# Planning the side work of an attention pass head by head

## The chip, the cores and the metric

The kernel runs on one core of a Trainium2 chip. The metric is the device time of one launch in microseconds, as the median of several runs; a profiled execution gives the trace. The engines are named as in the profile: PE is TensorE (matrix multiplications, with PEld its weight loads), DVE is VectorE, ACT is ScalarE, POOL is GpSimd, and SP is SyncE, which here only issues transfers (DMAs).

## The reference

One layer over 2048 tokens of 1024 channels in float32, with modulation vectors that come from a condition `c`:

```python
mod = (silu(c) @ w_mod).reshape(1, 6, 1, 1024)
sa, ca, ga, sb, cb, gb = (mod[:, i] for i in range(6))
h = layernorm(x) * (1 + ca) + sa
x = x + ga * A(h)                  # attention with memory
h = layernorm(x) * (1 + cb) + sb
x = x + gb * B(h)                  # MLP across the tokens, 3584 wide
```

`A` projects to q, k, v (32 heads of 32 channels) and cuts the tokens into 4 segments of 512. Within a segment each head has causal softmax attention; the state of the earlier segments (`M`, `z`) is read with `phi(q)` and mixed in by a gate `g`; then `M` and `z` take in the segment. The result is multiplied by `wo`.

```python
for s in range(4):
    a_dot = softmax(q_s @ k_s.T * scale + mask) @ v_s
    a_mem = (phi(q_s) @ M) / (phi(q_s) @ z + 1e-6)
    out_s = g * a_mem + (1 - g) * a_dot
    M, z = M + phi(k_s).T @ v_s, z + sum(phi(k_s))
```

## The kernel before

**Precision.** Float32 products are made from two reduced-precision parts. `split` writes a rounded high part and, by a subtraction, the low part; a product is three matmuls (high by high, high by low, low by high). A "page" is one 128 x 2 x 512 tile with both parts of one eighth of the channels of a segment; there are 16 pages, two segments' worth.

**The attention passes.** The heads are worked in groups of four (`NG` = 8 groups). An iteration `t` is one group in one segment; two passes (`pr`) take segments 0 and 1, then 2 and 3, and within a pass each group has its two segments in turn: 32 iterations, 128 heads. The loop at lines 560 to 588 runs over heads, `n` from -3 to 128. At `n` it traces `scores(n)` (three banks of score matmuls, exponentials on ScalarE, causal masks and the low half of the probabilities on GpSimd), `maxima(n + 3)` (scores in the other orientation, whose row maxima VectorE takes; after every second head small transfers, `sk<-nt`, place them as extra rows of the stacked operands), `values(n - 1)` (probabilities by values) and a quarter of the projections of the iteration two later (`project(n + 8)`), whose results are stacked by transfers `sk<-sg`.

**The side work** lies in the same loop and uses buffers `raw` (three of 128 x 1024):

- *Weights.* `load_w` (line 167) loads the q, k and v weights of a group, in three parts of 512 KB. In the first pass `load_part` splits them on ScalarE and VectorE into `w` tiles (eight buffers, six per group), and `keep_w` stores the split parts in `wsp` for the second pass, which only loads them.
- *Late token tiles.* `token_tile` (line 218, every fifth head from 4) loads one of token tiles 8 to 15 into a `raw` buffer, normalizes it, transposes it on TensorE through the `s2` banks, modulates it on ScalarE and stores it transposed in `hT1`. `reload_h` (line 297, loop index `m` = `n + 8` from 59 to 66) fetches it for segments 2 and 3, in 16 pieces, and splits each into a page on VectorE and GpSimd.
- *Late modulation.* `mod_late` (line 495) computes 128 of the 4096 remaining modulation values: it loads 128 rows of transposed weights and VectorE multiplies by `scb` with a sum along the row (1024 wide). It is traced every third head from 12, 32 times. `mod_rows` transposes the sums and stores them in `modd`, once after the first 8 (the attention gate) and once after the last.
- *Output weights.* `wo_ahead` (line 549), every fifth head from 66, loads an eighth of `wo`, multiplies it by the gate (`gaw`) on GpSimd, splits it on ScalarE and VectorE and stores the parts in `wos`; they are fetched into pages from head 115 on.

**Order.** The compiler's scheduler puts each engine's instructions in an order of its own by a model of their times. The order of tracing gives the priority, so an instruction that is traced later can be issued earlier when its engine is free in the model and its operands are there. An instruction under `tc.issue_after(i)` comes behind `i` if both are on one engine. At run time each engine works in that order.

After the loop come the output projection (`out_proj`), the second normalization and the token MLP with a seven-product scheme (`mix`), which the change does not touch.

Of the kernel before, what the change touches and what calls it, by code (L numbers as in the profile page):

```python
# [7 lines left out]
F32 = mybir.dt.float32  # L8
# [10 lines left out]
P = 128  # L19
# [15 lines left out]
ML0 = 12  # L35
MLS = 3
HB = 3
WO0 = 66
WOS = 5
# [5 lines left out]
def attention_and_mlp(ctx, tc, x, wq, wkv, wo, beta, w1, b1, w2, b2, c, wm_a, wm_b, out):  # L45
# [13 lines left out]
    hT1 = dram.tile([2, NK, P, L], F32, name="hT1")  # L59
# [87 lines left out]

    def load_part(g, pr, kind, part, res):


        if pr == 0:
            r = a.tile([P, D], F32, tag="raw", bufs=3, name=f"raw{kind}{g}_{part}")
            SY.dma_start(r, (wkv if kind == "v" else wq)[g, :, 1024 * part:1024 * part + 1024])
        for i in range(2):
            w = aw.tile([P, 2, 512], F32R, tag="w", bufs=8, name=f"w{kind}{pr}_{g}_{part}_{i}")
            if pr == 0:
                split(w, r[:, 512 * i:512 * i + 512], A, V)
            else:
                SY.dma_start(w.bitcast(F32), wsp[g, 2 * part + i if kind == "v" else 4 + i])
            res[kind, 2 * part + i] = w  # L160
# [251 lines left out]
    def maxima(t, h):  # L412
# [8 lines left out]
        for i, o in ((0, x[:, 0:128]), (2, x[:, 128:512]), (1, y[:, 0:256]), (3, z)):  # L421
            T.matmul(o, q[:, 128 * i:128 * i + 128], k[:, 0:128 * i + 128], start=True, stop=True)  # L422
            V.tensor_tensor_reduce(o, o, mask[:, 384 - 128 * i:], 1.0, -3.0e38, op0=ALU.add, op1=ALU.max,  # L423
                                   accum_out=mx[:, h % 2, i:i + 1])
# [7 lines left out]
        for hh in range(2):  # L432
            sk = d["sk", h - 1 + hh]
            for part in range(2):
                SY.dma_start(sk[96 + part:97 + part, 0].bitcast(F32).rearrange("p (b n) -> p b n", n=128),
                             nt[part][4 * hh:4 * hh + 4].bitcast(F32))

    def scores(t, h):
        d = st[t]
        q, k = d["sk", h][:, 0], d["sk", h][:, 1]  # L440
# [16 lines left out]
        A.copy(ph[:, 0], p32)  # L457
        G.tensor_tensor(ph[:, 1], p32, ph[:, 0], op=ALU.subtract)  # L458
# [36 lines left out]
    def mod_late(j):  # L495
# [450 lines left out]
```

## Time and profile before

| what | value |
|---|---|
| median of 3 runs | 2334.57 us (2332.73 to 2335.44) |
| the profiled execution | 2335.82 us |
| its span, first to last instruction | 2334.1 us |
| mean granted TensorE clock | 0.979 |
| first score matmul of heads 0, 48, 68 and 108 | 108.6, 484.8, 664.6 and 942.7 us |
| weight splits of groups 2 to 7 on VectorE (36) | 120.4 to about 470 us |
| late token tiles, loads | 109.7 to 390.1 us |
| late modulation on VectorE (32 steps) | 184.7 to 645 us |
| output weights, loads | 470.9 to 620.0 us |
| reload of token tiles, loads | 499.0 to 603.6 us |

How to read the rows: a group row names line, engine, operation, `written<-read` tiles, shapes and count, then after the bar the busy us and the mean ns of one, then the engine's idle time in front of them and what ended it. A row of waits has the total us, the number of waits and the longest. Rows of stretches give for each engine the busy us and the instruction count, then the granted clock, the DMA share and GB/s.

### The profile page before, as it was taken

What the parts mean: (1) busy time and instruction counts of PE and PEld (TensorE: products, weight loads), DVE (VectorE), ACT (ScalarE), POOL (GpSimd) and SP (SyncE); (2) the same over time, 40 slices, a digit from 0 to 9 for tenths busy, and PEclk for the clock granted to TensorE, in tenths of its full rate; (3) what the DMA queues carried; (4) which work ended last, traced back from release to release, by engine and by line L of the source; (5) the groups of instructions that cost most, each with busy time, mean ns of one, the idle gap of its engine ahead of it and who ended that gap; (6) DMA issues with size and microseconds to landing.
All of it is one profiled execution on the core that took longest, in us unless ns stands there. A gap on an engine that the chain in (4) does not pass through costs nothing.

```text
span 2334.1 us, 38271 instructions
## 1 busy us (share of the span) xinstructions
PE 2242.2 (96%) x13866; PEld 1925.3 (82%) x13866; DVE 1724.3 (74%) x3838; ACT 1103.8 (47%) x2002; POOL 683.7 (29%) x683
## 2 busy tenths in 40 slices
PE   8989999898899999998999999999999999999999
PEld 7878888887789999976887887888888788888887
DVE  6677777677766666665999665598889787868687
ACT  5476776655556666654434333353335242424232
POOL 3154544567655555554001000023332000000000
PEclk9999999999999999987999999999999999999999
DMA  6856666578744444483465765365557542423233
GB/s 244 251 152 185 175 187 186 161 240 263 244 119 119 119 122 120 109 264 98 132 217 187 271 235 195 136 246 222 211 213 275 185 136 71 146 65 130 68 114 148
DMA packets 164272, 406.27 MB, mean 174 GB/s; under 512 B 17108, under 2 KB 63220, under 8 KB 155124
## 3 DMA queue, kind: packets, MB, share of 16 engines
q1 hardware_dynamic: 164084, 403.83, 52.9%
q8 instruction: 110, 1.80, 0.3%
q14 instruction: 78, 0.64, 0.1%
HBM read 232.04 MB, written 120.86 MB: 151 GB/s over the span
## 4 chain that ended last, share of the span: by engine, by line
PE 82%; DVE 8%; DMA 6%; issue 2%; ACT 1%; SPq 1%; POOL 1%; DVEq 0%; ACTq 0%; POOLq 0%
PE mx L743 43%; PE nps L184 12%; PE po L650 8%; PE qps L192 7%; PE pv L472 3%; DMA rawm<-in_wm_b_dram 2%; PE sx L422 1%; PE sz L422 1%; PE a L444 1%; PE rd L394 1%; PE up L404 1%; PE a L447 1%; DVE bU L120 1%; PE a L451 1%; PE sy L422 1%
## 5 line engine op out<-in xcount | busy, mean ns | idle before, releaser
L743 PE MATMUL mx<-bU,sp 128*128 128x512 f32 x2352 | 535.9, 389 | 3.1 <-DVE ac L750 1.4
L743 PEld LDWEIGHTS mx<-bU,sp 128*128 128x128 f32 x2352 | 440.8, 188 | 97.8 <-issue 2.2
L184 PE MATMUL nps<-wv,h 128*128 128x256 f32 x3072 | 435.7, 284 | 4.7 <-DVE h L119 3.5
L743 PE MATMUL mx<-bA,sp 128*128 128x512 f32 x1764 | 431.8, 389 | 3.2 <-DVE cc L750 1.6
L117 ACT CAST sp<-wr 128x384 fp32r<-128x384 f32 (+2 forms) x408 | 217.4, 545 | 445.2 <-PE mx L743 373.7
L184 PEld LDWEIGHTS nps<-wv,h 128*128 128x128 f32 x3072 | 401.3, 190 | 10.1 <-DVE h L119 3.9
L743 PEld LDWEIGHTS mx<-bA,sp 128*128 128x128 f32 x1764 | 330.8, 188 | 73.6 <-DVE cc L750 2.0
L458 POOL TENSOR_TENSOR ph<-p,ph 128x1280 f16<-128x1280 f32 x128 | 344.7, 2693 | 145.2 <-ACT ph L457 144.9
L120 DVE TENSOR_TENSOR sp<-wr,sp 128x384 fp32r<-128x384 f32 (+2 forms) x408 | 259.1, 646 | 34.0 <-ACT sp L117 33.8
L750 DVE TENSOR_TENSOR ac<-mx,ac 128x512 f32<-128x512 f32 x280 | 189.8, 687 | 92.2 <-PE mx L743 91.5
L192 PE MATMUL qps<-h,wq 128*128 128x512 f32 x768 | 204.5, 413 | 3.8 <-DVE r L347 3.6
L650 PE MATMUL po<-wo,ots 128*128 128x512 f32 x768 | 180.7, 396 | 4.0 <-DVE ots L120 2.2
L455 POOL TENSOR_SCALAR_AFFINE_SELECT p<-p 128x256 f32<-128x256 f32 x256 | 123.9, 492 | 185.1 <-ACT p L448 83.1
L457 ACT CAST ph<-p 128x1280 f16<-128x1280 f32 x128 | 161.0, 1258 | 33.4 <-POOL p L455 33.1
L192 PEld LDWEIGHTS qps<-h,wq 128*128 128x128 f32 x768 | 147.8, 199 | 34.9 <-issue 3.9
L650 PEld LDWEIGHTS po<-wo,ots 128*128 128x128 f32 x768 | 146.6, 192 | 35.1 <-ACT ots L117 2.4
L423 DVE CUSTOM_DVE_ANT_0 sx<-sx,mask 128x128 f32<-128x128 f32 (+1 forms) x256 | 110.3, 431 | 77.1 <-PE sx L422 75.6
L743 PE MATMUL mx<-bB,sp 128*128 128x512 f32 x588 | 164.3, 389 | 0.0
L472 PE MATMUL pv<-vp,ph 128*128 128x97 bf16 (+1 forms) x2560 | 150.6, 206 | 8.4 <-DVE mv L131 4.8
L472 PEld LDWEIGHTS <-ph 128*128 128x128 f16 x2560 | 118.4, 100 | 33.0 <-issue 16.7
L750 DVE TENSOR_TENSOR cc<-mx,cc 128x512 f32<-128x512 f32 x140 | 94.8, 684 | 46.8 <-PE mx L743 43.9
L743 PEld LDWEIGHTS mx<-bB,sp 128*128 128x128 f32 x588 | 110.4, 188 | 22.9
(173 smaller groups left out, 3219.2 us busy)
## 6 DMA issues: line engine op xcount, KB each, us to landing
sk<-sg SPq DMA_DIRECT2D x384, 128.0 KB
wr<-in_w_dram SPq DMA_DIRECT2D x28, 1024.0 KB
wr<-in_w_dram SPq DMA_DIRECT2D x32, 768.0 KB
bstu<-ucd SPq DMA_DIRECT2D x28, 768.0 KB
wsp<-wv SPq DMA_DIRECT2D x32, 512.0 KB
rawm<-in_wm_b_dram SPq DMA_DIRECT2D x32, 512.0 KB
wv<-wsp SPq DMA_DIRECT2D x32, 512.0 KB
pcd<-cc SPq DMA_DIRECT2D x14, 1024.0 KB
```

What stands on the lines that cost most here:

```text
L117: A.copy(hi, src)
L120: lo_eng.tensor_tensor(lo, src, hi.bitcast(F32), op=ALU.subtract)
L184: T.matmul(ps[:, aa], h[:, j, 128 * tt:128 * tt + 128], wt[:, i, o:o + 256], start=(n == 0), stop=(n >= 6 * NK - 2), skip_group_check=True)
L192: T.matmul(ps, wt[:, i, o:o + 128], h[:, j], start=(k + n == 0), stop=(3 * k + n == 3 * NK - 1))
L423: V.tensor_tensor_reduce(o, o, mask[:, 384 - 128 * i:], 1.0, -3.0e38, op0=ALU.add, op1=ALU.max, accum_out=mx[:, h % 2, i:i + 1])
L455: G.affine_select(w, w, pattern=[[0, 2], [1, 128]], compare_op=ALU.is_ge, fill=0.0, base=0, channel_multiplier=-1)
L457: A.copy(ph[:, 0], p32)
L458: G.tensor_tensor(ph[:, 1], p32, ph[:, 0], op=ALU.subtract)
L472: T.matmul(pv[:, i, 0:w], ph[:, part, o:o + 128], d["vp"][:, j, h, 0:w], start=(n == 0), stop=(n == 19), skip_group_check=True)
L650: T.matmul(ps, os_[:, i, P * ct:P * ct + P], wop[ct, nh][:, j], start=(n == 0), stop=(n == 3 * NK - 1))
L743: T.matmul(ps, ops[q][:, i, P * k:P * k + P], b[:, j], start=(m == 0 and first), stop=(m == 3 * nk - 1), skip_group_check=True)
L750: V.tensor_tensor(d, ps, d, op=ALU.add)
```

## The change

Each piece of side work is divided into a load and its work, and both are given a head: `later(n, fetch, (m, step), ...)` puts the load at head `n` and each step at head `m`. At the end of the loop's body for `n`, the pieces of that head are traced under `behind(n)`: on ScalarE, GpSimd, VectorE and SP they come behind the last instruction of that head's own work on that engine (the cast of the probabilities, the low half, the last maximum, the last `sk<-nt` transfer). TensorE has no such mark.

| side work | load at head | work at head |
|---|---|---|
| token tile i (0 to 7), now loaded into `gaw` | 5i | 5i + 2 |
| weights of group g (2 to 7), from 8g - 16 on | + 1, + 3, + 5 | + 4, + 6, + 7 (store + 7) |
| modulation j (0 to 31) | 40 + 2j | 40 + 2j + 1 and + 2 |
| output weights i (0 to 7) | 65 + 6i | 65 + 6i + 2 |

The modulation step is four multiply-and-sum instructions of 256 columns, two at each head, and a reduction of the four sums. The multiplication, split and copy of the output weights go in halves. The token tiles are split before they are stored (copy on ScalarE, subtraction on GpSimd, two stores), `hT1` has both parts, and `reload_h` is one transfer of 512 KB into the page. The gate's row is spread over `gaw` at head 62, as before.

```diff
-    hT1 = dram.tile([2, NK, P, L], F32, name="hT1")
+    hT1 = dram.tile([2, NK, P, 2, L], F32, name="hT1")
...
+    def fetch_part(g, kind, part):
+        r = a.tile([P, D], F32, tag="raw", bufs=3, name=f"raw{kind}{g}_{part}")
+        SY.dma_start(r, (wkv if kind == "v" else wq)[g, :, 1024 * part:1024 * part + 1024])
+        return r
+
+    def split_part(g, kind, part, r):
+
+        for i in range(2):
+            w = aw.tile([P, 2, 512], F32R, tag="w", bufs=8, name=f"w{kind}0_{g}_{part}_{i}")
+            split(w, r[:, 512 * i:512 * i + 512], A, V)
+            W[0, g][kind, 2 * part + i] = w
...
     def token_tile(tt):
 
-        r = a.tile([P, D], F32, tag="raw", bufs=3, name=f"rawx{tt}")
-        SY.dma_start(r, x[P * tt:P * tt + P])
+        r = gaw
         norm_x(a, r)
...
+        hi = a.tile([P, D], F32, tag="raw", bufs=3, name=f"hix{tt}")
+        A.copy(hi.bitcast(F32R), r)
+        G.tensor_tensor(r.bitcast(F32R), r, hi, op=ALU.subtract)
         i = tt % 4
-        SY.dma_start(hT1[tt // 4 - 2, :, :, P * i:P * i + P].rearrange("k p n -> p k n"),
-                     r.rearrange("p (k n) -> p k n", k=NK))
+        for part, t in enumerate((hi, r)):
+            SY.dma_start(hT1[tt // 4 - 2, :, :, part, P * i:P * i + P].rearrange("k p n -> p k n"),
+                         t.rearrange("p (k n) -> p k n", k=NK))
...
     def reload_h(seg, ct):
-        t = pj.tile([P, L], F32, tag="tmp", bufs=2, name=f"hre{seg}_{ct}")
-        SY.dma_start(t, hT1[seg - 2, ct])
         pg = new_page(f"h{seg}_{ct}")
-        split(pg, t, V, G)
+        SY.dma_start(pg.bitcast(F32), hT1[seg - 2, ct])
         hpages[seg, ct] = pg
...
+    @contextmanager
+    def behind(n):
+
+        with ExitStack() as s:
+            for e in "AGVS":
+                if (n, e) in marks:
+                    s.enter_context(tc.issue_after(marks[n, e].ins))
+            yield
...
+    def mod_part(j, r, half):
+
+        if half == 0:
+            mpart[0] = const.tile([P, 4], F32, tag="mpart", bufs=2, name=f"mpart{j}")
+        for i in (2 * half, 2 * half + 1):
+            c = slice(256 * i, 256 * i + 256)
+            V.scalar_tensor_tensor(r[:, c], r[:, c], 1.0, scb[:, c], op0=ALU.mult, op1=ALU.mult,
+                                   accum_out=mpart[0][:, i:i + 1])
+        if half == 0:
+            return
+        V.tensor_reduce(mcol[:, j:j + 1], mpart[0], axis=AX.X, op=ALU.add)
...
+    def wo_split(i, r):
+
+        nh, c2 = i // 4, 2 * (i % 4)
+        hi = a.tile([P, 2, 512], F32, tag="raw", bufs=3, name=f"woh{i}")
+        for j in range(2):
+            G.tensor_tensor(r[:, j], r[:, j], gaw[:, 512 * nh:512 * nh + 512], op=ALU.mult)
+            A.copy(hi[:, j].bitcast(F32R), r[:, j])
+            V.tensor_tensor(r[:, j].bitcast(F32R), r[:, j], hi[:, j], op=ALU.subtract)
...
+    for j in range(32):
+        n = 40 + 2 * j
+        later(n, lambda j=j: mod_fetch(j), (n + 1, lambda r, j=j: mod_part(j, r, 0)),
+              (n + 2, lambda r, j=j: mod_part(j, r, 1)))
...
-        if 4 <= n < 44 and n % 5 == 4:
-            token_tile(8 + n // 5)
-        if n >= ML0 and (n - ML0) % MLS == 0 and (n - ML0) // MLS < 32:
-            mod_late((n - ML0) // MLS)
+        with behind(n):
+            for f in todo.pop(n, ()):
+                f()
```

More of the change, by code (lines that the diff above doesn't have):

```diff
@@ L146, in attention_and_mlp @@
     raw_w = {}
+    def fetch_part(g, kind, part):
[7 more added lines that the diff above has]
+            W[0, g][kind, 2 * part + i] = w
     def load_part(g, pr, kind, part, res):
         if pr == 0:
-            r = a.tile([P, D], F32, tag="raw", bufs=3, name=f"raw{kind}{g}_{part}")
-            SY.dma_start(r, (wkv if kind == "v" else wq)[g, :, 1024 * part:1024 * part + 1024])
+            split_part(g, kind, part, fetch_part(g, kind, part))
+            return
         for i in range(2):
             w = aw.tile([P, 2, 512], F32R, tag="w", bufs=8, name=f"w{kind}{pr}_{g}_{part}_{i}")
[L156 to L159, printed above, removed]
+            SY.dma_start(w.bitcast(F32), wsp[g, 2 * part + i if kind == "v" else 4 + i])
             res[kind, 2 * part + i] = w
@@ L575, in attention_and_mlp @@
             reload_h(seg, ct + 1)
-        if n == WO0 - 4:
-            spread(gaw, 0)
-        if n >= WO0 and (n - WO0) % WOS == 0 and (n - WO0) // WOS < 8:
-            wo_ahead((n - WO0) // WOS)
         if 4 * NI - 5 <= m < 4 * NI + 3:
```

60 lines of the change are left out of this document (42 added, 18 removed).

## The prediction

> **What bounds the kernel now.** I read the page first, then the busy time of the engines by stretches, then the groups and the waits of the two stretches that lose time, and last one stall in the timeline.
>
> ```profile
> span 2334.1 us, 38271 instructions
> PE 2242.2 (96%) x13866; PEld 1925.3 (82%) x13866; DVE 1724.3 (74%) x3838; ACT 1103.8 (47%) x2002; POOL 683.7 (29%) x683
> ```
>
> TensorE is busy for 96% of the span, so only its idle time and its slow clock can be won. Side work (weight splits, late token tiles, late modulation, output weights) runs beside the attention heads, so I cut the head loop where its density changes. Each row below is one stretch; the columns are its length, the busy time and instruction count of PE, PEld, DVE, ACT and POOL, the granted clock, the DMA share and GB/s. The second set counts the first score matmul of each head (line 444) alone, so its first x is the number of heads.
>
> ```profile
> 108.60:484.80 376.20, 346.92 (x2971) 313.32 (x2970) 277.40 (x771) 257.20 (x484) 189.72 (x188) 0.96 0.61 181
> 484.80:664.60 179.80, 158.24 (x1282) 140.89 (x1281) 135.58 (x352) 94.98 (x164) 126.65 (x106) 0.92 0.72 219
> 664.60:942.70 278.10, 278.00 (x2518) 256.64 (x2517) 168.06 (x587) 174.41 (x309) 155.81 (x179) 1.00 0.47 124
> ...
> 108.60:484.80 376.20, 21.32 (x48) 9.38 (x48) 0.96 0.61 181
> 484.80:664.60 179.80, 8.88 (x20) 4.06 (x21) 0.92 0.72 219
> 664.60:942.70 278.10, 17.48 (x40) 7.57 (x41) 1.00 0.47 124
> ```
>
> The third stretch (heads 68 to 107) has no side work: TensorE never rests, its clock is 1.00, and a head takes 278.10 / 40 = 6.95 us. That is the floor. The first stretch (heads 0 to 47) also transposes eight token tiles on TensorE:
>
> ```profile
> 108.60:484.80 376.20, 10.58 (x64) 8.03 (x64) 0.96 0.61 181
> ```
>
> So it loses 376.2 - 48 x 6.95 - 10.6 = 31.9 us, and the second (heads 48 to 67) 179.8 - 20 x 6.95 = 40.8 us. Together **72.7 us** are to be had; everything else in the change lies beside a busy TensorE.
>
> Who makes TensorE wait? First its waits, stretch one and then two, then those of VectorE for transfers (us in total, times, longest):
>
> ```profile
> PE sx L422 <- DVE mx L423: 14.7, 11, 3.8
> ...
> PE sx L422 <- DVE mx L423: 9.6, 6, 4.5
> ...
> DVE rawm L498 <- DMA rawm<-in_wm_b_dram: 10.7, 7, 3.3
> DVE st L125 <- DMA rawx<-in_x_dram: 4.1, 2, 2.1
> ...
> DVE rawm L498 <- DMA rawm<-in_wm_b_dram: 7.6, 7, 2.9
> DVE h L119 <- DMA hre<-hT: 2.9, 2, 1.9
> ```
>
> TensorE waits for VectorE's row maxima: the score banks of a later head come free late because VectorE, which works in order, stands behind side work, or behind side work whose data has not landed. The costliest stall, read in the timeline (start, duration, engine, line, and in brackets the idle time before):
>
> ```profile
> 635.70 1.38 SPq L497 DMA_DIRECT2D rawm<-in_wm_b_dram  x2
> ...
> 640.52 1.23 DVE L498 SCALAR_TENSOR_TENSOR rawm<-rawm,scb 128x1024 f32<-128x1024 f32 x1 [2.94 <-DMA rawm<-in_wm_b_dram]
> 640.76 3.45 POOL L458 TENSOR_TENSOR ph<-p,ph 128x1280 f16<-128x1280 f32 x1 [1.24 <-ACT ph L457]
> 641.87 3.42 DVE L498 SCALAR_TENSOR_TENSOR rawm<-rawm,scb 128x1024 f32<-128x1024 f32 x1
> 645.62 0.69 PE L422 MATMUL sx<-sk 96*128 96x384 f32 x1 [4.47 <-DVE mx L423]
> ```
>
> A load issued at 635.70 lands at 640.52 (4.8 us); VectorE waits 2.94 us for it, then a second modulation step, 1.23 us by itself, takes 3.42 us because GpSimd's subtraction runs at the same time. TensorE pays 4.47 us, and the clock afterwards.
>
> A stall costs more than its length:
>
> ```profile
> 494.00:508.00 14.00, 11.39 (x71) 9.46 (x70) 11.71 (x31) 7.76 (x15) 8.27 (x7) 0.76 0.61 187
> ...
> PE sy L422 <- DVE mx L423: 2.3, 1, 2.3
> ```
>
> In these 14 us the longest wait is 2.3 us, and the granted clock is 0.76. The Trainium skill, "TensorE: Matmul & The Clock Gate", section on HAM oscillation, says to keep TensorE's idle gaps under some 3.4 us. By that rule short stalls would cost no clock; this row shows 2.3 us costing it, so the measurement decides, and I let the clock part shrink only with the stalls.
>
> **The change part by part.** VectorE's load per head, busy plus its waits for transfers, is what I carry through: clean 168.06 / 40 = 4.20 us; stretch one (277.40 + 10.7 + 4.1) / 48 = 6.09; stretch two (135.58 + 7.6 + 2.9) / 20 = 7.30, above the 6.95 us that TensorE needs. The losses per head are 0, 0.66 and 2.04 us. The terms, from the groups of VectorE (busy us, mean ns), stretch one and then two:
>
> ```profile
> L498 DVE SCALAR_TENSOR_TENSOR rawm<-rawm,scb 128x1024 f32<-128x1024 f32 x18 | 26.1, 1448 | 10.7 <-DMA rawm<-in_wm_b_dram 10.7
> L120 DVE TENSOR_TENSOR wv<-rawv,wv 128x512 fp32r<-128x512 f32 x22 | 31.8, 1455 | 9.0 <-ACT wv L117 9.0
> L120 DVE TENSOR_TENSOR wq<-rawq,wq 128x512 fp32r<-128x512 f32 x12 | 12.8, 1074 | 0.6 <-ACT wq L117 0.6
> L498 DVE DVE_READ_ACCUMULATOR rawm<-rawm,scb 128x1 f32 x18 | 1.4, 80 | 0.0
> L556 DVE TENSOR_TENSOR wor<-wor,woh 128x1024 fp32r<-128x1024 f32 x1 | 1.2, 1216 | 0.0
> ...
> L498 DVE SCALAR_TENSOR_TENSOR rawm<-rawm,scb 128x1024 f32<-128x1024 f32 x14 | 23.2, 1660 | 7.6 <-DMA rawm<-in_wm_b_dram 7.6
> L119 DVE CAST h<-hre 128x512 fp32r<-128x512 f32 x16 | 17.8, 1110 | 2.9 <-DMA hre<-hT 2.9
> L556 DVE TENSOR_TENSOR wor<-wor,woh 128x1024 fp32r<-128x1024 f32 x8 | 12.7, 1587 | 2.2 <-ACT woh L555 2.0 <-DMA sk<-sg 0.2
> ```
>
> *Quarters.* The smallest and middle modulation step and the nearest shorter row of the same kind:
>
> ```profile
> L498 DVE SCALAR_TENSOR_TENSOR rawm<-rawm,scb x32: 1204/1226/3418, 184.7 to 641.9; 128x1024 f32<-128x1024 f32 x32
> ...
> L368 DVE SCALAR_TENSOR_TENSOR pq<-qps,rq 128x512 f32<-128x512 f32 x6 | 4.1, 688 | 0.8 <-ACT rq L366 0.7
> L475 DVE RECIPROCAL pv<-pv 128x4 f32<-128x4 f32 x46 | 8.7, 189 | 13.8 <-PE pv L472 13.8
> ```
>
> From 688 ns at 512 columns to 1226 at 1024 is 538 per 512, so 256 columns cost about 688 - 269 = 419 ns. Four, four reads of the accumulator (80 each) and a small reduction (bounded by the 189 ns row) are 2.19 us, against 1.31 now: 0.9 us more on each of 32. The means above the 1226 ns add up to 26.1 + 23.2 - 32 x 1.226 = 10.1 us of waiting for GpSimd. Quartered, that is between 10 us (one wait per step, as now) and 40 us (one per quarter); I take 20, nearer the low end since two quarters stand back to back. So 32 x 2.19 + 20 = 90 us, 2.8 us each. With steps every second head from 40 on, 4 fall in stretch one (now 18), 10 in two (now 14), 18 in three (now 0).
>
> *Stored split segments.* The 16 reloads lose VectorE's casts (17.8 + 2.9 us of waiting) and GpSimd's subtractions; each becomes one transfer straight into the page. In exchange each token tile gets a 1024-wide copy on ScalarE, a 1024-wide subtraction on GpSimd and a second store; the nearest rows are GpSimd's 1024-wide multiply (2510 ns) and the share of stretch one: 8 x 2.5 = 20 us on a GpSimd that is busy for 189.72 of 376.20, so at nothing; without that cover, 20 us at most.
>
> ```profile
> L120 POOL TENSOR_TENSOR h<-hre,h 128x512 fp32r<-128x512 f32 x16 | 20.5, 1279 | 7.7 <-DVE h L119 5.5 <-PE a L447 2.2
> L554 POOL TENSOR_TENSOR wor<-wor,gaw 128x1024 f32<-128x1024 f32 x7 | 17.6, 2510 | 8.4 <-DMA wor<-in_wo_dram 8.4
> ```
>
> *Output weights.* Now eight steps around heads 48 to 67, after it one there and seven later, in halves, about 1.6 us each as now. This also takes seven loads and their stores out of the stretch with the highest DMA share (0.72), more than the doubled reloads put in; so I cost the transfers at nothing there. In stretch three GpSimd takes 7 x 2.5 = 18 us on 155.81 of 278.10: at nothing, 18 us if that idle time is not where the steps fall. The orders at the ends hold: the gate's row is spread at head 62, six heads after its eighth modulation step; the last weights are stored about head 109 and fetched from 115; the last modulation rows (head 104) are needed after head 128.
>
> *Loads ahead.* Token tiles, weights and output weights get two or three heads, 14 to 21 us, against the 4.8 us landing: their waits go (4.1 us here). For modulation the lead is one head, less the time for which the load stands behind its head pair's small transfers on the SP queue: most of the 18.3 us should go, a fourth may stay (bounds 0 and 18.3).
>
> *Waits that the pins add.* Each side step is queued on VectorE, ScalarE, GpSimd and SP behind that head's own work, so nothing of the head waits for it; what is queued behind it is the next head's. On SP that is the stack transfers and the maxima's rows; a fetch that waits for one of three buffers holds them. TensorE's own cost of late rows is small now (bounds 0 and a repetition of it):
>
> ```profile
> PE a L444 <- DMA sk<-nt: 3.2, 3, 2.0
> ```
>
> *The sum.* Stretch one: 292.2 - 38.2 (18 steps with their waits) - 4.1 - 1.2 + 4 x 2.8 = 259.9, 5.41 us per head. Two: 146.1 - 31.9 - 20.7 - 12.7 + 10 x 2.8 + 1.6 = 110.4, 5.52. Three: 168.1 + 18 x 2.8 + 7 x 1.6 = 229.7, 5.74. Load to loss, two ways. Straight between the points (4.20, 0) and (6.09, 0.66): losses of 0.42, 0.46 and 0.54, in all 20 + 9 + 22 = 51 us. Bent through all three points (0.255 x squared - 0.133 x, x being the load above 4.20): 0.21, 0.27, 0.40, in all 10 + 5 + 16 = 31 us. The gain lies between 22 and 41 us. I take 35, nearer the bent line because only it goes through all three measured points. The profiled execution took 2335.8 us (span 2334.1 and 1.7 around it): 2335.8 - 35 = 2300.8; the median of the runs, 2334.57, lies 1.25 lower, so **2300 us**. A measurement of this kernel can tell about 0.2%, 4.7 us, from no change.
>
> **The rivals.**
>
> *All of the loss goes.* Evenly spread steps of half a microsecond fit between the maxima, no stall is left that slows the clock. For: VectorE's load stays below 83% of 6.95 everywhere. Against: the 22 + 12 weight splits stay, with their means of 1455 and 1074 ns. Gain 50 to 72 us: about 2274.
>
> *The load decides, the spacing doesn't.* The side work of VectorE is not less (quarters cost 29 us more), it only moves into 40 heads that have none. Modulation loads still land late, and the straight line holds or worse: gain 5 to 25, about 2319.
>
> *Slower: the quarters meet GpSimd in the clean heads.*
>
> ```profile
> L458 POOL TENSOR_TENSOR ph<-p,ph 128x1280 f16<-128x1280 f32 x43 | 113.6, 2642 | 47.1 <-ACT ph L457 47.1
> ```
>
> A half step stands right behind the maxima, where GpSimd's subtraction (2.64 us in each clean head, by this row) may just be running; the timeline above shows 2.2 us of such a wait. The 64 half steps are then 64 chances where there were 32. Price: TensorE's wait for the maxima averages 14.7 / 11 = 1.3 us in stretch one. Stretch one keeps its 31.9 us of loss, two falls to some 10 (the straight line's 9); if 40 of 64 half steps stall, 53 us are added: 95 against 72.7, about 2357. It decides from (72.7 - 42) / 1.3 = 23 stalling half steps. Against: of 32 whole steps now, the middle one shows 1226 ns, hardly more than the smallest. The Trainium skill, "SBUF — State Buffer", section "SBUF: two separate sides", says the port that VectorE and GpSimd share is held for a whole instruction and the other blocks fully. By that rule each quarter could wait for a whole subtraction; the 3.42 us step agrees, the middle of the 32 does not make it the usual case.
>
> *No effect.* If the compiler's order already was what the plan asks: the modulation ran from 184.7 to 641.9 us, and the plan reaches to head 106, so the order must change. Only a balance of gain and cost gives this.
>
> **How the numbers follow.** My forecast (2285 to 2310) has 0.42, all of the loss gone 0.20, the load deciding 0.16, within 4.7 us of now 0.05, slower 0.17. So faster 0.78, same 0.05, slower 0.17. The range: low end a gain of 67 us, 2268; high end 2338, into the slower case; about 0.04 and 0.14 stay outside.
>
> **What would show it.** Right: VectorE has no wait for x tiles or reloads, under 9 us for modulation; heads 48 to 67 take about 145 us; the clock there rises above 0.97; heads 68 to 107 take more than 278 us, about 294; modulation runs on until about head 106. Wrong: TensorE's waits for the maxima in the late heads exceed 30 us (slower), or new long waits of score matmuls for the small transfers show that the SP queue is blocked, or the weight splits of heads 0 to 47 still cost over 25 us.

## The result and the profile after

The changed kernel takes 2399.06 us (median, 2396.80 to 2407.14) against 2333.72 for the kernel before in the same comparison: ratio 1.0278, 95% interval 1.0263 to 1.0294. It is 65 us slower; the forecast was 35 us faster. The profiled execution took 2407.14 us. The page of the changed kernel, span, busy time and the two MLP matmul groups (busy us, mean ns):

```profile
span 2405.4 us, 38505 instructions
PE 2287.2 (95%) x13866; PEld 1937.0 (81%) x13866; DVE 1757.4 (73%) x4054; ACT 1111.5 (46%) x2018; POOL 672.0 (28%) x683
...
L810 PE MATMUL mx<-bU,sp 128*128 128x512 f32 x2352 | 550.3, 396 | 2.0 <-DVE sp L118 1.1
...
L810 PE MATMUL mx<-bA,sp 128*128 128x512 f32 x1764 | 443.0, 395 | 1.4 <-ACT cc L815 0.8
```

The same two groups on the page of the kernel before:

```profile
L743 PE MATMUL mx<-bU,sp 128*128 128x512 f32 x2352 | 535.9, 389 | 3.1 <-DVE ac L750 1.4
...
L743 PE MATMUL mx<-bA,sp 128*128 128x512 f32 x1764 | 431.8, 389 | 3.2 <-DVE cc L750 1.6
```

These matmuls belong to the token MLP, far behind the head loop, where the change edits nothing; yet each takes 6 to 7 ns longer, 14.4 + 11.2 = 25.6 us in all. The head loop by stretches (columns as in the prediction), changed kernel, heads 0 to 47, 48 to 67, 68 to 107 and 108 to 126:

```profile
109.30:513.20 403.90, 362.30 (x2962) 319.81 (x2960) 270.51 (x760) 262.04 (x488) 200.59 (x194) 0.92 0.51 149
513.20:677.50 164.30, 148.96 (x1275) 135.41 (x1272) 108.07 (x389) 89.23 (x160) 76.69 (x82) 0.95 0.68 211
677.50:993.20 315.70, 296.90 (x2599) 270.95 (x2597) 239.06 (x791) 185.99 (x329) 184.21 (x196) 0.98 0.61 177
993.20:1125.30 132.10, 116.84 (x934) 101.82 (x935) 73.68 (x249) 73.29 (x126) 75.13 (x82) 0.87 0.56 178
```

Against 376.2, 179.8 and 278.1 before, the first stretch is 27.7 us longer, the second 15.5 shorter, the third 37.6 longer. TensorE projects further ahead or less far at head 68, so the second and third are best read together: 480.0 against 457.9, +22.1. They hold 74 more of its matmuls than before (3874 against 3800), some 8 us at the pace of before (278.10 us for 2518); the last stretch has 55 fewer. In the first stretch 12.3 us of the 27.7 are more idle time of TensorE (403.90 - 362.30 against 376.20 - 346.92); in the other 15.4 it runs the same work at a lower clock (0.92 for 0.96). Behind the heads come 21.3 us. So the loss has three places, and the one behind the heads needs no theory about side work at all.

Waits in the head loop of the changed kernel, VectorE's for modulation loads (all heads up to 107) and ScalarE's in the token chain, that is, among the steps of a late token tile (heads 0 to 47); last, ScalarE's in the kernel before:

```profile
DVE rawm L529 <- DMA rawm<-in_wm_b_dram: 50.7, 26, 4.5
```

```profile
ACT gaw L212 <- DVE mv L211: 16.7, 6, 4.5
```

```profile
ACT rawx L206 <- DVE mv L205: 9.6, 4, 3.4
```

The first was 18.3 us before and was to go; it grew. The second was there before, but is new to the argument: ScalarE, which also makes the exponentials, stands waiting for VectorE's mean and variance of a token tile.

### The profile page after: what moved, and what is told of

It reads as the page before. It is cut to its first block, busy times and chain, and to the rows that moved or that the text cites. A ratio compares the mean times of both kernels' runs of the same rounds, so it can differ in the third digit from the quotient of the medians.

```text
span 2405.4 us, 38505 instructions
## 1 busy us (share of the span) xinstructions
PE 2287.2 (95%) x13866; PEld 1937.0 (81%) x13866; DVE 1757.4 (73%) x4054; ACT 1111.5 (46%) x2018; POOL 672.0 (28%) x683
## 4 chain that ended last, share of the span: by engine, by line
PE 79%; DVE 9%; DMA 6%; issue 2%; ACT 2%; SPq 1%; POOL 1%; DVEq 0%; ACTq 0%
PE mx L810 44%; PE nps L190 10%; PE po L717 7%; PE qps L198 7%; DMA rawm<-in_wm_b_dram 3%; PE pv L493 3%; DVE rawm L529 2%; PE sx L429 1%; PE a L465 1%; DMA sk<-nt 1%; PE sz L429 1%; PE up L411 1%; DVE sx L430 1%; PE scale L280 1%; PE rd L401 1%
## 5 line engine op out<-in xcount | busy, mean ns | idle before, releaser
L810 PE MATMUL mx<-bU,sp 128*128 128x512 f32 x2352 | 550.3, 396 | 2.0 <-DVE sp L118 1.1
L810 PE MATMUL mx<-bA,sp 128*128 128x512 f32 x1764 | 443.0, 395 | 1.4 <-ACT cc L815 0.8
L717 PEld LDWEIGHTS po<-wo,ots 128*128 128x128 f32 x768 | 146.9, 192 | 35.6 <-ACT ots L115 5.1
L493 PE MATMUL pv<-vp,ph 128*128 128x97 bf16 (+1 forms) x2560 | 145.0, 206 | 9.0 <-DVE red L500 5.0
L817 DVE TENSOR_TENSOR cc<-mx,cc 128x512 f32<-128x512 f32 x140 | 94.9, 684 | 59.7 <-PE mx L810 55.6
```

Of the source, the lines that this page charges most:

```text
L493: T.matmul(pv[:, i, 0:w], ph[:, part, o:o + 128], d["vp"][:, j, h, 0:w], start=(n == 0), stop=(n == 19), skip_group_check=True)
L717: T.matmul(ps, os_[:, i, P * ct:P * ct + P], wop[ct, nh][:, j], start=(n == 0), stop=(n == 3 * NK - 1))
L810: T.matmul(ps, ops[q][:, i, P * k:P * k + P], b[:, j], start=(m == 0 and first), stop=(m == 3 * nk - 1), skip_group_check=True)
L817: V.tensor_tensor(d, ps, d, op=ALU.add)
```

## The experiments

Lengths of the stretches in us, each from the run's profiled execution, cut at the first score matmul of the heads (summed over the trace; the rows that carry the verdicts follow in their places). Apart from the first five rows (before, changed, e2, e12, e7), every row is the changed kernel on the addresses of before, with the named pins left ("pins": the engines in `behind`). A profiled execution lies up to 9 us off the median of its runs (e9 below it, e11 above), so a few us between two rows say nothing.

```text
run                          heads 0-47   48-107   108-126   after   median of runs
before                          376.2      457.9     132.6   1258.8      2333.7
changed kernel                  403.9      480.0     132.1   1280.1      2399.1
e2  before, shifted 64 B        377.8      460.2     132.4   1280.8      2361.5
e12 before, shifted 128 B       377.1      458.1     132.6   1280.0      2361.6
e7  before, split segments      370.9      461.8     129.3   1256.3      2332.5
e1  all four pins               396.9      477.2     129.5   1252.2      2372.4
e4  ScalarE VectorE GpSimd      411.0      465.2     129.1   1252.2      2371.1
e6  ScalarE GpSimd              408.6      473.7     129.6   1254.3      2376.2
e10 ScalarE                     413.7      479.1     136.5   1256.3      2397.0
e13 ScalarE, token tiles only   404.6      466.9     131.6   1259.0      2376.2
e14 ScalarE, all but tokens     370.2      479.6     141.6   1257.5      2359.5
e16 ScalarE, mark earlier       387.9      475.1     135.8   1254.4      2367.0
e17 VectorE GpSimd SP           378.8      484.0     134.5   1254.3      2365.4
e3  none                        368.0      470.5     131.1   1253.6      2336.8
e5  VectorE                     374.3      465.7     131.2   1254.4      2334.3
e11 GpSimd                      370.3      471.2     126.8   1250.2      2323.6
e8  none, whole steps           361.0      459.8     130.4   1258.1      2320.5
e9  VectorE, whole steps        370.3      448.1     136.0   1252.8      2325.0
e15 VectorE GpSimd, whole steps 373.9      454.0     130.4   1252.4      2320.0
e18 GpSimd, whole steps         360.2      456.9     126.7   1255.3      2310.2
```

### Addresses: e1, e2, e12

The only thing of the change that reaches the MLP is where tiles lie: the new partial sums, two tiles of 16 bytes per partition padded to 64 bytes in all, sit in the first pool on the left of the memory and push every later tile of that side up, among them `sp`, which these matmuls read, while `bU` and `bA`, on the right, stay. e1 takes the sums from an old tile that is not used any more; e2 and e12 push the tiles of the kernel before.

```diff
# e1, on the changed kernel
-    const.tile([P, 8], F32, name="offset")
+    offset = const.tile([P, 8], F32, name="offset")
...
-            mpart[0] = const.tile([P, 4], F32, tag="mpart", bufs=2, name=f"mpart{j}")
+            mpart[0] = offset[:, 4 * (j % 2):4 * (j % 2) + 4]
# e2, on the kernel before (e12: four tiles)
+    for i in range(2):
+        V.memset(const.tile([P, 4], F32, tag="shift", bufs=2, name=f"shift{i}"), 0.0)
```

> The changed kernel with its four-column tiles for the partial sums taken out of a tile that was there before, so that every on-chip address is as in the kernel before (in the changed kernel all tiles that grow from the left lie 64 bytes higher, those from the right side don't). Theory 1, addresses: the 128x512 matmuls of the MLP go back from 233 to 227 ns, the part after the head loop from 1280 to 1259 us, in all 20 to 24 us off 2399, about 2377. Rival: the MLP is slower for a reason of its own (a clock, a different order of instructions): no change, 2399.

> The kernel before with two small tiles (16 bytes each, 64 with padding) put where the changed kernel has its partial sums, and cleared once: all left-hand addresses rise by 64 bytes, nothing else changes. Theory 1, addresses: 20 to 28 us above 2334, about 2357, nearly all of it behind the head loop. Rival: 2334.

> The kernel before with all left-hand addresses 128 bytes higher (four cleared tiles in place of two; 64 bytes gave 2361.5 against 2336). If the distance to the right-hand tiles counts step by step: slower again than 2361, 2375 or more. If it is a matter of place within some line of 128 bytes or less: back at 2336. If any move off the present place costs the same: 2361.

e1 takes 2372.39 us, ratio 1.0158 (1.0141 to 1.0174): 26.7 less than the changed kernel. e2 takes 2361.52, 1.0106 (1.0091 to 1.0121), and e12 2361.63, 1.0107 (1.0092 to 1.0122): the kernel before pays the same for two idle tiles, and 128 bytes cost what 64 do. The page of e2:

```profile
L745 PE MATMUL mx<-bU,sp 128*128 128x512 f32 x2352 | 550.6, 396 | 2.0 <-DVE sp L120 1.1
...
L745 PE MATMUL mx<-bA,sp 128*128 128x512 f32 x1764 | 443.1, 395 | 1.4 <-ACT cc L750 0.8
```

The same 395 and 396 ns without any of the change's work (394 and 395 in e12). And in e1, with all of the change's work on the addresses of before, the 389 ns are back:

```profile
L810 PE MATMUL mx<-bU,sp 128*128 128x512 f32 x2352 | 535.4, 389 | 2.9 <-DVE sp L118 1.7
```

A stretch inside the MLP, changed kernel, then the kernel before:

```profile
1350.00:1750.00 400.00, 400.00 (x1721) 322.67 (x1720) 282.56 (x383) 144.84 (x236) 51.12 (x32) 1.00 0.55 205
```

```profile
1300.00:1700.00 400.00, 398.40 (x1758) 329.58 (x1757) 284.12 (x390) 147.09 (x240) 54.31 (x33) 1.00 0.57 212
```

400 us hold 1721 matmuls instead of 1758 (232 against 228 ns from one to the next), at a granted clock of 1.00 in both, and the slower one has no idle time at all: it is neither the throttle nor a wait. So some 26 of the 65 us are settled, and e1 is the base for what follows.

### The pins, one set at a time: e3, e4, e5, e6, e10, e11

```diff
# each with e1's edit
-            for e in "AGVS":
+            for e in "":       # e3; e4 "AGV", e5 "V", e6 "AG", e10 "A", e11 "G", e17 "GVS"
```

> The changed kernel with the old addresses and without the pins: the side pieces are traced at the same heads, but nothing holds them behind that head's own work. Theory 2, the pins: they put each modulation load on SP behind its head pair's small transfers, and so make it late (VectorE waits for it rose from 18.3 to 50.6 us): 20 to 35 us below the run with old addresses, about 2347, with VectorE's waits for modulation loads under 25 us. Rival, the placement: side work in heads 68 to 107 and the later plan cost what they cost, pinned or not: within 8 us of it.

> The changed kernel with the old addresses and the pins on VectorE, ScalarE and GpSimd, but not on SP, so that loads may be issued ahead of the small transfers. Theory 2 in its narrow form (the SP pin alone makes the loads late): 15 to 30 us below the run with old addresses, VectorE's waits for modulation loads under 25 us. If the pins on the computing engines are what costs: no change here but a gain in the run without pins. Rival, placement: within 8 us of it in both.

> Old addresses, pins on VectorE alone (2372 with all pins, 2337 with none). Theory A, the pins on ScalarE and GpSimd cost (a weight's copy behind the cast of the probabilities is late, VectorE's subtraction stands and waits for it, and the stacked transfers follow late): about 2340. Theory B, the pin on VectorE costs (side steps can no longer fill the gaps before the maxima but stand right behind them, in front of the next head's): about 2370. In between if both cost.

> Old addresses, pins on ScalarE and GpSimd alone. Theory A: about 2370, with heads 0 to 47 at 390 us or more. Theory B: about 2340.

> Old addresses, quarters, the pin on ScalarE alone. Theory: a weight part's high copy behind the cast of the probabilities starts VectorE's subtraction while GpSimd, released by the same cast, runs its subtraction of 2.6 us, and the two can't run at once. Then 2365 to 2378 (2337 without pins), the weight subtractions on VectorE at a mean of over 1250 ns (800 without pins). Rival, the GpSimd pin (order on GpSimd) costs: about 2338 here.

> Old addresses, quarters, the pin on GpSimd alone. Theory (ScalarE's pin costs): 2332 to 2342, weight subtractions near 800 ns. Rival: 2365 or more.

Without pins the time is that of before: 2336.79, ratio 1.0002 (0.9993 to 1.0012). So the pins cost e1 its 36 us, and quarters, stored segments and the new tracing together bring nothing. Without pins, however, the compiler's order does not keep the plan's heads: e3's modulation steps run from 400.5 to 720.4 us, those of the changed kernel from 469.7 to 967.8. That the late heads are not what costs is shown by e5 and e11, where they run to 928.1 and 908.5 us. VectorE's pin alone changes nothing (e5, 0.9987, 0.9974 to 1.0001), GpSimd's alone brings 13 us (e11, 0.9946, 0.993 to 0.9962), ScalarE's alone costs 60 (e10, 1.0253, 1.024 to 1.0267), with GpSimd's 39 (e6, 1.0168, 1.0149 to 1.0186). e4, without SP's, was to gain 15 to 30 us on e1 and in its total looks like it (1.0147, 1.0132 to 1.0162). The first stretch of e10 and ScalarE's waits in it, then both of e3:

```profile
111.00:524.70 413.70, 371.36 (x2954) 328.88 (x2953) 264.31 (x784) 261.51 (x487) 198.35 (x194) 0.89 0.53 151
```

```profile
ACT gaw L212 <- DVE mv L211: 20.4, 7, 4.7
```

```profile
113.40:481.40 368.00, 344.55 (x2962) 315.37 (x2961) 256.10 (x825) 256.87 (x485) 201.93 (x194) 0.95 0.64 184
```

```profile
ACT gaw L212 <- DVE mv L211: 7.0, 3, 2.9
```

The engines do nearly the same work; ScalarE's waits in the token chain are three times as long and the clock falls from 0.95 to 0.89.

### Which of ScalarE's steps: e13, e14, e16

```diff
# e13 (e14: the other way round); each step carries `token`
...
-        with behind(n):
-            for f in todo.pop(n, ()):
+        for f in todo.pop(n, ()):
+            f, token = f if isinstance(f, tuple) else (f, False)
+            with behind(n, "A" if token else ""):
# e16: ScalarE's pin alone, its mark at the third exponential
-        A.activation(p32[:, 896:1280], b2_[:, 0:384], AF.Exp, scale=SCALE, bias=shift)
+        marks[n, "A"] = A.activation(p32[:, 896:1280], b2_[:, 0:384], AF.Exp, scale=SCALE, bias=shift)
...
-        marks[n, "A"] = A.copy(ph[:, 0], p32)
+        A.copy(ph[:, 0], p32)
```

> Old addresses, quarters, the pin on ScalarE for the eight token tiles alone (2337 without pins, 2397 with ScalarE's pin on all). Theory T: ScalarE, in order, stands in the token chain (waits for VectorE's statistics rose from 7.0 to 20.4 us) right behind the cast, in front of the next head's exponentials, and the score banks come free late: 2360 or more here. Rival W, the copies of weights cost: within 8 us of 2337.

> Old addresses, quarters, the pin on ScalarE for all but the token tiles (weight parts, output weights). Theory W: the copy right behind the cast sends VectorE's subtraction into GpSimd's, and pushes the next exponentials by 1.2 us: 2360 or more, weight subtractions over 1050 ns. Theory T: within 8 us of 2337.

> As the run with the pin on ScalarE alone (2397), but behind the third exponential of the head, one instruction ahead of the cast, so that side work can use ScalarE's wait for GpSimd's mask and is not released together with GpSimd's subtraction. If the place behind the cast is what costs: 2345 or less. If any pin to a head on ScalarE costs: over 2375.

Token tiles alone cost 39 us (e13, 2376.18, 1.0174, 1.0155 to 1.0192), the rest 23 (e14, 2359.49, 1.0097, 1.0078 to 1.0116); 39 + 23 is about e10's 60. So each theory had a part of it, and neither had it alone. The table shows where: each run with the token steps pinned behind ScalarE's cast needs 397 to 414 us for heads 0 to 47, each run without that pin 360 to 379. The waits of e13 show the chain again, and its timeline shows ScalarE between the last exponential of one head (L473) and the first of the next (L466):

```profile
ACT gaw L212 <- DVE mv L211: 18.5, 8, 4.1
```

```profile
298.57 0.58 ACT L473 ACTIVATE p<-a,shift 128x384 f32<-128x384 f32 x1 [3.68 <-PE a L472]
...
304.83 1.25 ACT L212 ACTIVATE gaw<-gaw,mv 128x1024 f32<-128x1024 f32 x1 [0.51 <-DVE mv L211]
308.48 2.91 ACT L235 ACTIVATE gaw<-hpl,saca 128x128 f32<-128x128 f32 x8 [2.40 <-PE hpl L232]
311.49 1.11 ACT L238 CAST hix<-gaw 128x1024 fp32r<-128x1024 f32 x1
312.60 0.69 ACT L466 ACTIVATE p<-a,shift 128x512 f32<-128x512 f32 x1
```

The whole token chain stands between two heads, 14 us from one exponential to the next. Summed over the traces, the eight heads with a token tile's work last 10.1 us each in e3 and 19.3 in e13; the other 40 of the first stretch get part of it back (7.2 and 6.3). What is not shown is why this delay costs and another does not: with VectorE's pin alone the eight heads last 15.8 us and the others 6.2, and e5's total is no worse than e3's. TensorE's own waits in the first stretch of e13 name VectorE (23.5 us) more than ScalarE (9.9), and 24 of the 37 us between e3 and e13 are longer busy time of TensorE, at a granted clock of 0.91 instead of 0.95, and not idle time.

For the weights I held the split itself for the cause. The groups of VectorE's subtraction (mean ns after the bar), e1, with GpSimd's subtraction of the probabilities beside it; then e3, e14 and e16:

```profile
L118 DVE TENSOR_TENSOR wv<-rawv,wv 128x512 fp32r<-128x512 f32 x32 | 43.0, 1367 | 6.8 <-ACT wv L115 6.8
...
L479 POOL TENSOR_TENSOR ph<-p,ph 128x1280 f16<-128x1280 f32 x128 | 340.9, 2664 | 149.7 <-ACT ph L478 149.5
```

```profile
L118 DVE TENSOR_TENSOR wv<-rawv,wv 128x512 fp32r<-128x512 f32 x32 | 25.1, 802 | 16.2 <-ACT wv L115 16.0
```

```profile
L118 DVE TENSOR_TENSOR wv<-rawv,wv 128x512 fp32r<-128x512 f32 x32 | 38.8, 1231 | 3.1 <-ACT wv L115 3.0
```

```profile
L118 DVE TENSOR_TENSOR wv<-rawv,wv 128x512 fp32r<-128x512 f32 x32 | 25.2, 810 | 6.4 <-ACT wv L115 6.4
```

With its copy pinned behind ScalarE's cast, the subtraction starts just when that cast has released GpSimd's 2.66 us, and takes 1231 to 1367 ns instead of 802; with the mark one instruction earlier (e16) it is back at 810. The Trainium skill, "SBUF — State Buffer", section "SBUF: two separate sides", says that on the port pair that VectorE and GpSimd share the instruction that starts first keeps it to its end; these rows agree. But the time does not hang on it: e14 has the slow subtractions and needs 370.2 us for heads 0 to 47, e3 368.0. Its 20 us lie behind head 48 (479.6 + 141.6 against 470.5 + 131.1), where ScalarE's pinned side work is nearly all output weights' copies. Why these should cost so much is open. e16 itself (2367.0, 1.0133, 1.0108 to 1.0158) lies between its two forecasts: it saves half of e10's 60 us, of which 413.7 - 387.9 = 25.8 in heads 0 to 47.

### ScalarE's pin undone, the others kept: e17

> The changed kernel with only two things undone: the partial sums lie in an old tile (the addresses of before) and ScalarE has no pin; VectorE, GpSimd and SP keep theirs, the quarters and the split segments stay. Theory (the loss is ScalarE's pin and the addresses, the rest of the change costs little): between 2325 and 2340 us, near the version without pins (2337) or that with VectorE's alone (2334), so about the time of before. Rival (the pins of the other three engines together cost what none of them costs alone): 2350 or more. If GpSimd's pin gives its 13 us here too: 2324.

2365.41 us, 1.0131 (1.0113 to 1.015): the theory failed and the rival held. The first stretch does give back what ScalarE took (396.9 to 378.8), but heads 48 to 107 take 484.0 us. Heads 48 to 67 and 68 to 107 of e17 and VectorE's waits in both; then heads 0 to 47, 48 to 67 and 68 to 107 of e5, which has VectorE's pin alone:

```profile
488.60:653.10 164.50, 150.00 (x1282) 136.68 (x1277) 113.73 (x391) 90.60 (x158) 76.71 (x83) 0.96 0.66 205
653.10:972.60 319.50, 294.17 (x2550) 268.98 (x2549) 236.18 (x784) 180.97 (x324) 180.89 (x191) 0.97 0.60 174
```

```profile
DVE rawm L529 <- DMA rawm<-in_wm_b_dram: 54.5, 24, 5.8
```

```profile
109.60:483.90 374.30, 347.14 (x2953) 312.47 (x2951) 258.04 (x762) 260.21 (x489) 198.13 (x194) 0.95 0.58 169
483.90:643.50 159.60, 148.88 (x1286) 136.03 (x1287) 113.74 (x392) 89.47 (x160) 81.59 (x86) 0.97 0.66 202
643.50:949.70 306.20, 292.05 (x2543) 265.20 (x2541) 234.73 (x778) 180.92 (x325) 182.22 (x195) 0.97 0.62 180
```

VectorE's busy time is the same within 1.5 us, TensorE's within 3.3; TensorE's idle time is 39.8 us against 24.9. e17's 24 waits of VectorE for modulation loads there add up to 54.5 us; e5 has one such wait in its whole run:

```profile
DVE rawm L529 <- DMA rawm<-in_wm_b_dram: 0.8, 1, 0.8
```

One of e17's in the timeline (start, duration, engine, line):

```profile
531.05 0.58 SPq L518 DMA_DIRECT2D rawm<-in_wm_b_dram  x1
531.74 0.62 SPq L323 DMA_DIRECT2D sk<-sg  x1
...
535.76 1.73 DVE L529 SCALAR_TENSOR_TENSOR rawm<-rawm,scb 128x256 f32<-128x256 f32 x1 [4.41 <-DMA rawm<-in_wm_b_dram]
537.43 0.61 DVE L529 SCALAR_TENSOR_TENSOR rawm<-rawm,scb 128x256 f32<-128x256 f32 x1
537.97 0.61 DVE L529 SCALAR_TENSOR_TENSOR rawm<-rawm,scb 128x256 f32<-128x256 f32 x1
538.51 0.42 DVE L529 SCALAR_TENSOR_TENSOR rawm<-rawm,scb 128x256 f32<-128x256 f32 x1
538.96 0.40 DVE L354 TENSOR_TENSOR r<-nps,vp 128x256 f32<-128x256 f32 x1
539.41 0.69 PE L361 MATMUL kps<-ident,k 128*128 128x128 f32 x2 [4.41 <-DVE r L354]
```

The load is issued at 531.05, VectorE reaches the step at once and waits 4.41 us, and all four quarters, of which two were meant for the next head, stand in front of a subtraction that TensorE's projection needs: it pays 4.41 us as well. Summed over the traces, the step comes 4.5 us after its load's issue in e17 and 4.4 in e1, the two with SP's pin (medians of 32), and VectorE had been ready for it after 3.0 and 3.1 us. Where VectorE is pinned and SP is not, it comes after 22.2 us (e5) and 16.5 us (e4), and VectorE does not wait for most of the loads. So SP's pin takes away the lead that the plan gives on paper: it holds the load behind the small transfers of a head while VectorE's pin lets the step go. The price in heads 48 to 107 is 477.2 - 465.2 = 12 us from e1 to e4, which differ in SP's pin alone. From e17 to e5 it is 484.0 - 465.7 = 18, but these differ in GpSimd's pin too. A third pair says the same: e15 below has the pins of VectorE and GpSimd and whole modulation steps, and needs 454.0 there; whole steps are worth 10.7 (e3 to e8) to 17.6 (e5 to e9) of the 30.0 to e17, which leaves 12 to 19 for SP's pin if the parts add. e4 did not show it in its total, because its heads 0 to 47 took 14 us longer than e1's. SP's pin was not tried alone, and why the first stretch of e4 gives the gain back is open.

### Quarters: e8, e9, e15, e18

```diff
# no half steps; e8 no pins, e9 "V", e15 "GV", e18 "G"
-            V.scalar_tensor_tensor(r[:, c], r[:, c], 1.0, scb[:, c], op0=ALU.mult, op1=ALU.mult,
-                                   accum_out=mpart[0][:, i:i + 1])
...
+        V.scalar_tensor_tensor(r, r, 1.0, scb, op0=ALU.mult, op1=ALU.mult, accum_out=mcol[:, j:j + 1])
```

> Old addresses, no pins (2337), the modulation step whole (one instruction of 1024 columns, planned two heads behind its load) in place of four quarters and a reduction. If quarters cost what I priced (0.9 us each on VectorE and up to 30 us of waits for GpSimd): 5 to 20 us below, about 2325. If their shortness saves stalls: 5 to 15 us above. If neither: within 4 us.

> Old addresses, the pin on VectorE alone, whole modulation steps. If the two findings add up (quarters cost 16 us in 2337 -> 2320, the VectorE pin -2.5): about 2318, and under the 2336 of the kernel before. If the pin with whole steps (1.3 us and more right behind the maxima) stalls TensorE: above 2325.

> Old addresses, pins on VectorE and GpSimd, none on ScalarE and SP, whole modulation steps. Alone, from 2337: GpSimd's pin -13, VectorE's -2.5, whole steps -16. If they add up: about 2305. If the order is a matter of chance among small differences: 2315 to 2330. Under 2336 in both cases.

> GpSimd's pin alone and one modulation step of 1024 columns, on the addresses of before. If the two gains add (13 us from GpSimd's pin, 16 from the whole steps, off 2337): about 2307, below 2315. If they are gains from the same waits: about 2320, as for the version without pins and for that with three pins, both with whole steps.

The whole step stands two heads behind its load, where the first two quarters stood one behind. Without pins, whole steps take 2320.46 us (e8, 0.9931, 0.9916 to 0.9947): quarters cost 16. The groups of e18 and, quartered, of e11, both with GpSimd's pin alone:

```profile
L527 DVE SCALAR_TENSOR_TENSOR rawm<-rawm,scb 128x1024 f32<-128x1024 f32 x32 | 46.1, 1442 | 23.7 <-DMA rawm<-in_wm_b_dram 23.7
```

```profile
L529 DVE SCALAR_TENSOR_TENSOR rawm<-rawm,scb 128x256 f32<-128x256 f32 x128 | 71.3, 602 | 15.3 <-DMA rawm<-in_wm_b_dram 15.3
```

25.2 us more for the same product, not counting 96 more reads of the accumulator. With VectorE's pin whole steps bring 9 us (e9, 2324.95, 0.9944, 0.993 to 0.9959; 2318 was forecast), with two pins the time is that of none (e15, 2320.0, 0.993, 0.991 to 0.995, so the gains do not add there), and with GpSimd's alone they nearly add: e18 takes 2310.18, ratio 0.9898 (0.9881 to 0.9916), 26.6 of 13 + 16 us below e3 and the fastest version here. That it has 23.7 us of waits for loads shows that such waits need not cost; in e17's timeline an instruction that TensorE needs stands behind one.

### Stored split segments alone: e7

The kernel before with the two-part `hT1`, the two stores and the reload straight into the page, and nothing else of the change.

> The kernel before with the token tiles stored already split and reloaded by one transfer, all else as before (addresses too). My prediction's term: heads 48 to 67 lose VectorE's 17.8 us of casts and 2.9 us of waits, some 15 us off, nothing lost elsewhere: about 2320. Rival: the copy, the subtraction and the second store of each token tile in heads 0 to 47 take as much as the reload gives: 2334 within 5.

2332.49 us, 0.9983 (0.9974 to 0.9993): a gain of 3.3 us (1.6 to 6.1 by the interval), where 15 were expected. Heads 48 to 67 and 68 to 107 in e7:

```profile
481.60:659.10 177.50, 157.15 (x1287) 139.59 (x1285) 126.20 (x335) 93.48 (x163) 102.71 (x90) 0.91 0.76 237
659.10:943.40 284.30, 281.86 (x2559) 260.78 (x2557) 188.75 (x608) 176.67 (x313) 161.28 (x182) 1.00 0.49 133
```

VectorE and GpSimd are lighter in the first of these by 9.4 and 23.9 us than before, and its length falls by 2.3; the next is 6.2 longer, with 41 more of TensorE's matmuls in it. TensorE's idle time in the two is 22.8 us, and was 21.7. The work was taken away, and TensorE's stalls did not go with it.

## Why the prediction was wrong

**The floor and the loss.** 6.95 us per head and 72.7 us to be had stand. By the same count the changed kernel loses 59.7, 25.3 and 37.7 us in the three stretches, 122.7; some 8 us of this are the 74 matmuls that lie there earlier than before.

**"Everything else lies beside a busy TensorE", and all behind the loop counted as unchanged.** Failed by 26 us (e1, e2): a new tile of a few bytes moved the MLP's operands. No step of the prediction looked at what the allocation shifts.

**"Waits that the pins add": nothing of the head waits for it.** This is the step that cost most. Its working looked only at SP's small transfers (0 to 3.2 us). What it called "the next head's" is what TensorE needs next: ScalarE stands in order in the token chain before the next exponentials (39 us for tokens alone by e13, and 18 of e1's, 396.9 to 378.8 in heads 0 to 47), and SP's pin takes the lead from the modulation loads (12 to 19 us in heads 48 to 107, though e4's total gives only 1 us back). That these pins cost is shown; the way from the late exponentials to TensorE's slower clock is argued.

**"Loads ahead".** Its condition, "less the time for which the load stands behind its head pair's small transfers", was the right one, and its size wrong: in the changed kernel VectorE was ready for the step 3.1 us after the load's issue (median; 6.0 before), sooner than the 4.8 us that the load of the prediction's timeline took, and the waits rose from 18.3 to 50.7 us instead of falling below 9. Waits for token tiles were not gone either (3.8 us in the changed kernel, 7.0 in e17). The new waits were not on the list of what would make it slower: TensorE's for late maxima in heads 48 to 107 stayed at 18.1 us, since part of the cost goes through other VectorE steps, as at 539.41 in e17's timeline; in all it waited 30.5 us for VectorE there.

**Quarters.** The price on VectorE was right: the middle one of 128 takes 421 ns where 419 was estimated, and they are busy for 73.3 us, 19.4 above 128 x 0.421, where 20 was taken (in e5, with VectorE's pin alone, 92.1 us):

```profile
L529 DVE SCALAR_TENSOR_TENSOR rawm<-rawm,scb x128: 365/421/2918, 469.7 to 967.8; 128x256 f32<-128x256 f32 x128
```

What they cost in time was not: 16 us by e3 and e8, 9 by e5 and e9, 13 by e11 and e18.

**Load to loss.** The two curves that turned VectorE's load into loss fell with e5. Its load in heads 0 to 47 is 258.04 / 48 = 5.4 us per head and a little waiting, where 5.41 was forecast; the bent line gave a loss of 10 us, the straight one 20, and the stretch loses 374.3 - 333.6 - 10.6 = 30.1, as before the change (31.9). In heads 48 to 107 the forecast losses were 21 to 31 us, and e5 loses 48.7. e7 says the same. Three points from stretches with different work made a curve, but the load was not its cause. What the timelines point to instead is which instruction stands in front of the one that TensorE waits for.

**The stretches named as signs.** Heads 48 to 67 took 164.3 us (145 forecast) at a clock of 0.95, heads 68 to 107 took 315.7 (294). Modulation ran to 967.8 us, about head 105 (106 forecast). The sign against the forecast, weight splits that still cost over 25 us in heads 0 to 47, came true: their 34 subtractions kept VectorE busy for 53.1 us, against 44.6 before, and the stretch lost 59.7 us.

**The rivals.** The slower one (2357) had a real mechanism, the shared port, and its 20 us of longer quarters; but the quarters' 9 to 16 us are a quarter of the loss at most. The rival of the load had modulation loads that still land late, without SP's pin as the reason, and expected a gain all the same. None named ScalarE's order or the addresses.

**What stays open.** Why a shift of 64 or 128 bytes lengthens these matmuls; what costs e14 its 20 us behind head 48; why all four pins cost less than ScalarE's alone; and why the stored segments alone bring 3 us of 15. Each pin also changes the order that the compiler finds for the other engines, and a difference of some 10 us, such as GpSimd's 13, may come from that and not from the pin; no run tells the two apart. In steps the loss is: addresses 26.7 us (changed kernel to e1), the four pins 35.6 (e1 to e3), and 0.7 for all the rest (e3 to before), in which quarters cost 16 and the other edits bring about as much (e8, without quarters, takes 15 less than before); together 63 of the 65, which come from another comparison. How the 35.6 are divided is less sure: e1 to e17 and e1 to e4 each give back little in total, and e10 shows that the pins' costs do not simply add.

## What to carry to other kernels

An order that pins side work behind a head's own work is not free: on an engine that works in order, each wait inside the side work stands in front of the next head. It suggests pinning only steps whose operands are already there, and not pinning a load on its queue as tightly as the step that uses it; no run here tried such a plan as a whole. Price an edit by the instruction that it delays, not by an engine's average load. And when a kernel gets slower, compare first a stretch that the change does not touch: here it held 21 of the profiled 71 us, and putting the addresses back was worth 27.

## What the runs showed of the hardware

A matmul with 512 columns of float32 operands took 394 to 396 ns instead of 389 when one operand's tiles lay 64 or 128 bytes higher and the other's did not; in the changed kernel it came every 232 instead of 228 ns, at a granted clock of 1.00. An instruction of VectorE of 802 ns took 1367 in the mean when an order put it beside one of GpSimd of 2.66 us. And in the prediction's 14 us of the kernel before, one short gap went ahead of a slow clock: TensorE is busy up to 498.4 us at a granted clock of 1.00, stands for 2.30 us, and is granted 0.50 from 502 to 506 us.
